# Moving seven small loads to other queues, adding three filler products, and a new hand-off order in an S5 scan and MLP kernel

## The chip, the cores and the metric

The kernel runs on one core of one Trainium2 chip. A core has four compute engines that run their own instruction streams: TensorE (PE, matrix products into PSUM), VectorE (DVE), ScalarE (ACT) and GpSimd (POOL). A fifth, SyncE (SP), only issues transfers and waits. Transfers between the device's memory and the on-chip buffer are issued from the stream of SP, ACT or POOL and carried by DMA engines. Engines meet at semaphores. The metric is the device time of one execution in microseconds; the median of several executions is compared.

## The reference, cut to what matters

```python
xn = layernorm(x)                                   # x: 1 x 2048 x 448, bfloat16
# A: a diagonal complex recurrence over the 2048 positions
Lam_bar = exp(exp(log_dt) * Lam);  B_bar = ((Lam_bar - 1) / Lam)[:, None] * Bmat
Bu = einsum("bld,pd->blp", xn, B_bar)
h[t] = Lam_bar * h[t-1] + Bu[t]
s = 2 * real(einsum("blp,dp->bld", h, Cmat)) + xn * Dskip
# B: an MLP over a second layernorm
g = silu(gelu(layernorm(xn) @ w1 + b1) @ w2 + b2)   # w1: 448 x 1792, w2: 1792 x 448
out = x + s * g
```

## The kernel before, in words

The 2048 positions are cut into four groups of 512 (g0 to g3), each of two blocks of 256. For each group the kernel makes the two normalised inputs (transposed by DMA into `xnT` for the scan and `xn2T` for the MLP), the first MLP product with w1 and its GELU (`mm1_phase`, lines 650 to 670, the GELU on ACT at line 668), the second with w2 and its SiLU (`mm2`, lines 778 to 790), the scan's input products (`bu_phase`, 679 to 722), the scan itself on DVE (`ssm`, 736 to 770), the scan's output products (`yt`, 794 to 829) and the sum with x (`out_dma`, `out_pe`). The contraction over 448 rows is done in 64-row halves that run side by side in the PE.

The first group is special. Its MLP products run for block 0 as soon as x's first rows have come (`first_stats`, `first_apply`), and for block 1 after that, in pieces of 256 columns; a pair of PSUM banks holds two of w1's column blocks, there are three such pairs, and ACT has to apply the GELU to a pair before the PE can fill it again. Ahead of the first products the PE runs filler products on constants (`dummies`, lines 376 to 378: `n` products of `cols` columns into a bank that nobody reads) and a few tiny products that turn rows of parameters into columns: `parameters` (475, 476), `b1_columns` (549, 550) and `skip_columns` (555, 556, which takes the rows of D and b2 that are loaded at line 355).

w1 is loaded in four column chunks (`ldw1`, 335 to 339): rows 0 to 383 of a chunk, then the remainder, rows 384 to 447, as a DMA of its own, and a copy `w1c` of a part of it to other partitions. All of them are issued by SP in the kernel before, and so are the rows of D and b2.

What runs where and when is written out. Every operation is a numbered task of a `Plan`, in the order in which the program adds it. `ORDER` (line 154) is a hand-off order of all task numbers; each engine's stream is that list with the other engines' tasks left out, and a task waits only for the tasks whose data it needs (`emit`, 99 to 146). So an engine that waits at the head of its stream holds everything behind it. Some tasks may run on either of two engines (`either`, 65 to 70: `small` is GpSimd or VectorE, `copy` is ScalarE or VectorE); those whose numbers stand in `SECOND` (line 174) take the second one.

Places that the prediction's steps use: `ln_scale` (416 to 434, the scale and offset of a group's layernorm: ten short chained operations on DVE, or five with a power on GpSimd), `ln_apply` (436 to 445, lines 443 on DVE and 444 on ACT), the sine of the parameters (`sine`, 492 to 498, ten short chained operations), `tables` (564 to 584: range reduction of the rotation table at 566 to 570, its absolute value at 572, five sines on ACT at 580, the decay table `dk` at 583), `lb` (609 to 616) and `bt` (618 to 622), which make and transpose the scan's input matrices `BT`, and `combine` (588 to 597).

Of the kernel before, what the change touches and what calls it, by code (L numbers as in the profile page):

```python
# [148 lines left out]
def dram_ap(t, offset, ap):  # L149
    return bass.AP(tensor=t.tensor, offset=offset, ap=ap)  # L150
# [1 line left out]


ORDER = [int(k) for k in """
# [18 lines left out]
""".split()]  # L173
SECOND = [int(k) for k in """
26 29 32 56 60 69 83 90 113 115 172 173 175 177 178 180 181 182 202 204 205 207 208 209 210 212 214 216 218 220 222 234 236 238 240 244 246 256 258
270 277 278 280 324 338 349 360 361 364 365 409 443 444 445 446 471 472 473 474 475 487 489 527 528 529 542 549 551 560 575
""".split()]


# [18 lines left out]
def bass_recurrent_scan__ssm_conv_s5__mixer_channel_mlp__prompt_kernel(  # L198
# [11 lines left out]
    L, D, F = 2048, 448, 1792  # L210
# [6 lines left out]
    with ExitStack() as es:  # L217
        def SB(name, shape, dtype=BF):
            return es.enter_context(nc.sbuf_tensor(name, shape, dtype))
# [12 lines left out]
        w1_sb = SB("w1_sb", [128, 4, F])  # L232
# [9 lines left out]
        drows = vrows[64:66, 64:512]  # L242
# [54 lines left out]
        def pe(fn, reads=(), writes=(), split=False):  # L297
            kb.add("pe", fn, reads, writes, split=split)

        def copy(pairs, rd, wr):  # L300
            kb.either(("act", [lambda e, o=o, i=i: e.activation(o, i, ACT.Copy) for o, i in pairs]),  # L301
                      ("dve", [lambda e, o=o, i=i: e.tensor_copy(o, i) for o, i in pairs]), rd, wr)

        with nc.Block():
# [17 lines left out]
            def ld(eng, o, i, writes, reads=()):  # L322
                kb.dma(eng, o, i, reads=reads, writes=writes)
# [4 lines left out]
            def ldx(b0, n, reads=()):  # L328
                ld("sp", x_all[:, b0:b0 + n, :, :], dram_ap(A_x, b0 * 256 * D, [[2 * D, 128], [256 * D, n], [D, 2], [1, D]]),
                   [f"x{b}" for b in range(b0, b0 + n)], reads)  # L330
# [4 lines left out]
            def ldw1(c):  # L335
                a, w = CH[c][0] * 128, CH[c][1] * 128
                ld("sp", w1_sb[:, 0:3, a:a + w], dram_ap(B_w1, a, [[F, 128], [128 * F, 3], [1, w]]), [f"w1_{c}"])
                ld("sp", w1_sb[64:128, 3, a:a + w], dram_ap(B_w1, 384 * F + a, [[F, 64], [1, w]]), [f"w1r_{c}"])
                copy([(w1_sb[0:64, 3, a:a + w], w1_sb[64:128, 2, a:a + w])], [f"w1_{c}"], [f"w1c_{c}"])

            for par in range(2):
                ld("sp", x_all[:, 0, par, :], dram_ap(A_x, par * D, [[2 * D, 128], [1, D]]), [f"x0p{par}"])
            ldx(1, 1)
            ldw1(0)
            ld("act", brows[0:3, :], dram_ap(B_b1, 256, [[512, 3], [1, 512]]), ["br0"], ["br"])
            ld("act", brows[3:4, 0:256], dram_ap(B_b1, 0, [[256, 1], [1, 256]]), ["br1"], ["br"])
            for c in range(1, 4):
                ldw1(c)
# [3 lines left out]
            for c, (a, n) in enumerate(CH):  # L352
                ld("sp", w2_sb[:, a:a + n, :], dram_ap(B_w2, a * 128 * D, [[n * D, 128], [D, n], [1, D]]), [f"w2_{c}"])
            for i, vec in enumerate((A_Dskip, B_b2)):
                ld("sp", drows[i:i + 1, :], dram_ap(vec, 0, [[D, 1], [1, D]]), [f"dbr{i}"])
            ldx(2, 2)
            def xk(b):
                return [f"x{b}"] if b else ["x0p0", "x0p1"]
# [17 lines left out]
            def dummies(n, rd=(), bank=3, cols=256):  # L376
                wide = nc.const_aps.tensor_like(1.0, xn_sb[:, 0, 0:cols])
                pe([lambda e: e.matmul(psum[:, bank, 0:cols], one, wide, start=True, stop=True) for _ in range(n)], list(rd), [f"ps{bank}"])
# [169 lines left out]
            def b1_columns():  # L548
                pe([lambda e, k=k: e.matmul(psum[:, 4, 2 + k:11 + k:4], brows[0:4, k:512:4], ident[32:36, 32:35], start=True, stop=True) for k in range(4)]
                   + [lambda e, k=k: e.matmul(psum[:, 4, k:k + 1], brows[0:4, k:256:2], ident[32:36, 35:36], start=True, stop=True) for k in range(2)],  # L550
                   ["br", "br0", "br1", "ident"], ["ps4"])
                copy([(b1f[:], psum[:, 4, 0:14])], ["ps4"], ["b1f"])
# [119 lines left out]
            def mm1_run(g, b, js, pairs):  # L672
                for j in js:
                    mm1_phase(g, b, j, pairs[j - js[0]], False)
                    if j > js[0]:
                        mm1_phase(g, b, j - 1, pairs[j - 1 - js[0]], True)
                mm1_phase(g, b, js[-1], pairs[js[-1] - js[0]], True)
# [205 lines left out]
            dummies(1, ["st0"])  # L883
            first_apply(0)
            b1_columns()
            mm1_run(0, 0, range(6), (0, 1, 2, 0, 1, 2))
            first_apply(1)
            mm1_run(0, None, range(6, 7), (0,))
# [83 lines left out]
```

## Time and profile before

| | us |
|---|---|
| median of three executions without a profile | 148.27 (147.64 to 148.87) |
| the profiled execution, its own time | 148.68 |
| its span, from the first instruction to the last | 146.9 |
| TensorE busy in the span | 140.0 (95%) |
| VectorE busy | 130.7 (89%) |
| ScalarE busy | 102.8 (70%) |
| GpSimd busy | 23.9 (16%) |

The time of an execution is the span and 1.8 us around it. Rows of the profile give a start and a duration in us, the engine (PEld is the PE's load of weights, SPq and ACTq are issues of transfers), the line of the kernel, the operation, the tiles as out<-in and a count; in brackets stands the idle time of the engine before it and what ended that. In a table of windows, each engine has its busy time and the number of its instructions, then come the PE's granted clock, the busy share of the DMA engines and the rate of transfers.

### The profile page before, as it was taken

What the parts mean: (1) busy time and instruction counts of PE and PEld (TensorE: products, weight loads), DVE (VectorE), ACT (ScalarE), POOL (GpSimd) and SP (SyncE); (2) the same over time, 40 slices, a digit from 0 to 9 for tenths busy, and PEclk for the clock granted to TensorE, in tenths of its full rate; (3) what the DMA queues carried; (4) which work ended last, traced back from release to release, by engine and by line L of the source; (5) the groups of instructions that cost most, each with busy time, mean ns of one, the idle gap of its engine ahead of it and who ended that gap; (6) DMA issues with size and microseconds to landing.
All of it is one profiled execution on the core that took longest, in us unless ns stands there. A gap on an engine that the chain in (4) does not pass through costs nothing.

```text
span 146.9 us, 3570 instructions
## 1 busy us (share of the span) xinstructions
PE 140.0 (95%) x1421; PEld 90.2 (61%) x1427; DVE 130.7 (89%) x284; ACT 102.8 (70%) x188; POOL 23.9 (16%) x83
## 2 busy tenths in 40 slices
PE   7789999999999999999999999999999999999990
PEld 2577774454455485466758555887775668564860
DVE  2989999999587999999999999496999999999891
ACT  3667999988799766999989773615768997064200
POOL 2630777710000000060500000000000600000000
PEclk9977999999999999999999999999999999999998
DMA  4799996999589791000000018917440010005404
GB/s 114 219 253 275 393 230 127 167 251 184 105 170 230 146 112 35 2 4 0 4 0 0 0 22 160 212 38 147 84 155 0 0 63 4 18 0 107 182 10 125
DMA packets 38850, 15.98 MB, mean 109 GB/s; under 512 B 33193, under 2 KB 38450, under 8 KB 38834
## 3 DMA queue, kind: packets, MB, share of 16 engines
q1 hardware_dynamic: 38276, 15.52, 47.6%
q10 hardware_dynamic: 558, 0.24, 0.6%
q8 instruction: 11, 0.18, 0.5%
q14 instruction: 5, 0.04, 0.1%
HBM read 5.86 MB, written 1.84 MB: 52 GB/s over the span
## 4 chain that ended last, share of the span: by engine, by line
PE 86%; ACT 4%; SPq 2%; DMA 2%; issue 1%; DVE 1%; DVEq 0%
PE psum L662 28%; PE psum L784 24%; PE psum L691 14%; PE psum L806 7%; PE psum L807 6%; PE psum L787 4%; ACT gT L668 3%; SPq L78 2%; DMA w_sb<-in_B_w_dram 2%; PE psum L814 2%; ACT xn_sb L444 1%; DVE Bn L862 1%; ACT tmp L595 0%; PE psum L815 0%; PE psum L856 0%
## 5 line engine op out<-in xcount | busy, mean ns | idle before, releaser
L662 PE MATMUL psum<-xn2T,w_sb 64*128 64x512 bf16 (+1 forms) x476 | 48.3, 349 | 0.7 <-DMA w_sb<-in_B_w_dram 0.4
L668 ACT ACTIVATE gT<-psum,b1f 128x512 bf16<-128x512 f32 (+1 forms) x68 | 37.3, 615 | 4.9 <-PE psum L662 3.9
L784 PE MATMUL psum<-gT,w_sb 128*128 128x512 bf16 x162 | 36.3, 379 | 0.6 <-issue 0.3
L662 PEld LDWEIGHTS psum<-xn2T,w_sb 64*128 64x128 bf16 x476 | 26.5, 111 | 16.6 <-PE psum L662 1.9
L784 PEld LDWEIGHTS psum<-gT,w_sb 128*128 128x128 bf16 x168 | 16.2, 98 | 18.9 <-issue 0.6
L691 PE MATMUL psum<-xnT,BT 64*128 64x256 bf16 x392 | 24.4, 269 | 0.0
L691 PEld LDWEIGHTS psum<-xnT,BT 64*128 64x128 bf16 x392 | 18.8, 94 | 6.2 <-issue 0.8
L790 ACT ACTIVATE g_sb<-psum,db 128x512 bf16<-128x512 f32 (+1 forms) x16 | 9.8, 627 | 10.2 <-PE psum L787 4.6
L750 DVE TENSOR_TENSOR_SCAN s_w<-vs,dk 128x1048 f32<-128x1048 bf16 (+1 forms) x8 | 16.4, 2061 | 0.2
L444 ACT ACTIVATE xn_sb<-x_all,lnw 128x448 bf16<-128x448 bf16 (+2 forms) x20 | 13.2, 696 | 0.1
L827 DVE SCALAR_TENSOR_TENSOR tmp<-xnT,db,psum 128x512 f32<-128x512 bf16 (+1 forms) x17 | 10.8, 650 | 2.5 <-PE psum L815 1.8
L301 ACT ACTIVATE vs<-s_w 64x258 bf16<-64x258 f32 (+2 forms) x11 | 6.5, 611 | 6.7 <-DVE s_w L750 6.6
L806 PE MATMUL psum<-hx,CZ 128*128 128x256 bf16 x84 | 10.9, 275 | 0.0
L807 PE MATMUL psum<-Bn,CQ 128*128 128x256 bf16 x84 | 10.8, 273 | 0.0
L466 ACT ACT_TABLE_LOAD x8 | 10.3, 1283 | 0.3
L301 ACT ACTIVATE ue<-psum 128x512 bf16<-128x512 f32 (+1 forms) x14 | 7.1, 548 | 4.5 <-PE psum L691 4.5
L806 PEld LDWEIGHTS psum<-hx,CZ 128*128 128x128 bf16 x84 | 8.0, 98 | 2.4 <-ACT u_sb L301 0.4
L807 PEld LDWEIGHTS psum<-Bn,CQ 128*128 128x128 bf16 x84 | 8.0, 98 | 1.6 <-issue 0.4
L829 DVE TENSOR_TENSOR t<-tmp,g_sb 128x512 bf16<-128x512 f32 (+1 forms) x14 | 8.4, 626 | 0.0
L301 ACT ACTIVATE u_sb<-psum 128x256 bf16<-128x256 f32 (+1 forms) x14 | 6.1, 508 | 2.8 <-PE psum L691 2.8
L443 DVE TENSOR_SCALAR xn_sb<-x_all,lnw 128x384 bf16<-128x384 bf16 (+2 forms) x20 | 6.1, 353 | 1.8 <-ACT xn_sb L444 1.7
L364 DVE BATCH_NORM_STATS2 lnst<-x_all 128x6 f32<-128x448 bf16 x12 | 7.0, 614 | 0.0
(158 smaller groups left out, 174.4 us busy)
## 6 DMA issues: line engine op xcount, KB each, us to landing
x_all<-in_A_x_dram SPq DMA_DIRECT2D x3, 448.0 KB, 4.7
w_sb<-in_B_w_dram SPq DMA_DIRECT2D x3, 448.0 KB, 7.1
out_dram<-Bn SPq DMA_DIRECT2D x6, 224.0 KB, 2.9
w_sb<-in_B_w_dram SPq DMA_DIRECT2D x3, 384.0 KB, 4.3
Bn<-in_A_B_im_dram SPq DMA_DIRECT2D x1, 336.0 KB, 7.6
Bn<-in_A_B_re_dram SPq DMA_DIRECT2D x1, 336.0 KB, 7.9
x_all<-in_A_x_dram SPq DMA_DIRECT2D x2, 112.0 KB, 2.1
x_all<-in_A_x_dram SPq DMA_DIRECT2D x1, 224.0 KB, 2.6
```

The source lines that it names most:

```text
L301: kb.either(("act", [lambda e, o=o, i=i: e.activation(o, i, ACT.Copy) for o, i in pairs]), ("dve", [lambda e, o=o, i=i: e.tensor_copy(o, i ...
L444: ("act", [lambda e, o=o, i=i: e.activation(o, i, ACT.Identity, bias=nb, scale=rs) for o, i in parts]),
L466: kb.add("act", lambda e: e.preload_act_table_set(what), reads, writes, sem=name)
L662: return lambda e: e.matmul(dst(bk[k]), w1_sb[rows, d, fcol(2 * j + k)], rhs[rows, d], start=not second and n == 0, stop=second and n == 3)
L668: act(lambda e, k=k, fi=fi: e.activation(gT[:, gb, fi, cols], psum[:, bk[k], cols], ACT.Gelu_apprx_tanh, bias=b1f[:, fi:fi + 1]), ["b1f", ...
L691: fns.append(lambda e, rows=rows, bank=bank, m=m, o=o, n=n: e.matmul(psum[:, bank, c * NK:(c + 1) * NK].rearrange("p (b c) -> p b c", b=2) ...
L750: dve(lambda e, so=so, vi=vi, di=di: e.tensor_tensor_scan(so, vi, di, 0.0, ALU.add, ALU.mult), ["v", "vl", "vz", "dk", "dk01"] + ["v3"] * ...
L784: pe([lambda e, fi=fi: e.matmul(psum[:, bk, :], w2_sb[:, fi, 128 * j:128 * j + 128], gT[:, gb, fi, :], start=fi == 0, stop=fi == NF - 1) f ...
L790: act(lambda e: e.activation(g_sb[:, gb, 512 * j:512 * j + n], psum[:, bk, 0:n], ACT.Silu, bias=b2c[:, j:j + 1]), [f"ps{bk}", "db", f"Ws{g ...
L806: pe([lambda e, k=k: e.matmul(par(psum[:, bk, :], 1), CZ[:, k, cols], halves(hx[:, hb, k, 1:NK + 1]), start=k == 0, stop=k == 6) for k in ...
L807: fns = [lambda e, k=k: e.matmul(par(psum[:, bk, :], 0), CQ[:, k, cols], halves(hz[:, hb, k, :]), start=not by_pe and k == 0, stop=not by_ ...
L827: dve([lambda e, o=o, p=p, x=x, d=d: e.scalar_tensor_tensor(out=v(o), in0=x, scalar=d, in1=v(p), op0=ALU.mult, op1=ALU.add) for o, p, x, d ...
```

## The change

Three edits are written in the code, and the two lists are new.

```diff
-                ld("sp", w1_sb[64:128, 3, a:a + w], dram_ap(B_w1, 384 * F + a, [[F, 64], [1, w]]), [f"w1r_{c}"])
+                ld("act", w1_sb[64:128, 3, a:a + w], dram_ap(B_w1, 384 * F + a, [[F, 64], [1, w]]), [f"w1r_{c}"])
...
-                ld("sp", drows[i:i + 1, :], dram_ap(vec, 0, [[D, 1], [1, D]]), [f"dbr{i}"])
+                ld("pool", drows[i:i + 1, :], dram_ap(vec, 0, [[D, 1], [1, D]]), [f"dbr{i}"])
...
             b1_columns()
+            dummies(3, cols=512)
             mm1_run(0, 0, range(6), (0, 1, 2, 0, 1, 2))
...
 ORDER = [int(k) for k in """
-9 11 16 17 18 44 14 15 13 42 24 10 22 12 4 23 360 2 93 94 95 96 97 106 0 101 1 45 92 105 107 46 47 98 111 49 41 99 102 25 50 19 20 100 66 27 34 110 3
...
+2 3 11 25 14 15 5 0 12 44 10 6 13 9 4 1 45 16 93 94 22 95 23 17 18 24 19 96 97 106 46 98 20 99 48 41 111 101 92 105 100 47 107 108 109 42 53 36 28 112
...
 SECOND = [int(k) for k in """
-26 29 32 56 60 69 83 90 113 115 172 173 175 177 178 180 181 182 202 204 205 207 208 209 210 212 214 216 218 220 222 234 236 238 240 244 246 256 258
...
+21 26 29 32 48 50 57 59 60 63 66 73 75 76 80 83 85 89 90 110 173 177 179 180 182 203 204 206 209 210 211 213 215 217 219 221 223 232 235 237 241 243
...
```

The added filler task has number 116, so a task that had a number from 116 on now has the next one. With that taken into account the lists differ as follows, as far as the prediction speaks of it.

- ScalarE's stream: the remainder of w1's chunk 1 is its first issue, ahead of the three rows of parameters; the remainder of chunk 0 comes behind the second pair of logarithm and exponential of `first_stats`, those of chunks 2 and 3 right after the exponential of log_dt. SP's stream keeps w1's upper rows, in the order chunk 1, 0, 2, 3.
- GpSimd's stream: the rows of D and b2 are issued behind its constants. It gets the `ln_scale` of group 0 (before on VectorE), further down that of group 2, and two more of the four products of the identity with D (line 562).
- From ScalarE to VectorE: the copies of w1's chunk 0 (`w1c_0`) and of the first transposed half block, two of the four `ln_apply` of group 0's scan input. From VectorE to ScalarE: the copy of the second transposed half block, the column b1, one `ln_apply` of group 1's MLP input.
- From GpSimd to VectorE: the sine of the parameters, the wrap before it (`wrap`, 489 to 491) and a dozen short operations on parameters; four such go the other way.
- ScalarE's absolute value (line 501) stands ahead of the first GELU instead of behind the eighth. Behind the last GELU of group 0 it has first one `ln_apply` of group 1 (line 444), then the SiLU table, then the absolute value of line 572.
- VectorE's stream: the copies of w1's chunks 1 and 2, `dk` and one of the four operations of line 570 come later; the third is behind the `ln_scale` of group 1.
- SP's stream: x's blocks 4 and 5 are issued behind the transposes of `xnT` for group 0 instead of ahead of them; the three transposes of `BT` come in the order 2-5-6, 0-3, 1-4 with a load of x in between.
- The PE's stream up to group 1's second product is the same but for the filler products; from there on neighbouring tasks change places in some thirty spots. In the last group the output's block 3 comes last instead of block 2.

More of the change, by code (lines that the diff above doesn't have):

```diff
@@ L154 @@
 ORDER = [int(k) for k in """
[18 rows of a table removed]
[18 rows of a table added]
 """.split()]
 SECOND = [int(k) for k in """
-26 29 32 56 60 69 83 90 113 115 172 173 175 177 178 180 181 182 202 204 205 207 208 209 210 212 214 216 218 220 222 234 236 238 240 244 246 256 258
-270 277 278 280 324 338 349 360 361 364 365 409 443 444 445 446 471 472 473 474 475 487 489 527 528 529 542 549 551 560 575
+21 26 29 32 48 50 57 59 60 63 66 73 75 76 80 83 85 89 90 110 173 177 179 180 182 203 204 206 209 210 211 213 215 217 219 221 223 232 235 237 241 243
+245 247 249 257 261 271 272 277 279 281 323 339 340 352 353 365 366 430 444 445 446 447 473 474 475 488 490 530 531 543 550 561 576
 """.split()]
```

34 rows, old and new, of the table ORDER are left out of this document.

## The prediction

> **What bounds the kernel now.** I began with the chain of waits, to see where the time lies before the PE is fed without a break; then the windows of half a microsecond over the start, then ScalarE's timeline. The chain in order of time, rows with start and length:
>
> ```profile
> 4.67 3.47 DMA w_sb<-in_B_w_dram
> ...
> 18.53 3.03 PE psum L662 x50
> 21.57 0.16 issue
> 21.73 9.01 PE psum L784 x41
> 30.74 1.65 PE psum L787 x28
> 32.39 6.22 PE psum L662 x55
> ```
>
> The first products of the MLP wait until 8.14 for the small remainder of w1's chunk 0, the ninth transfer that SP issues. The first GELU stage keeps the PE until 21.57; from 21.73 to 32.39 the second product of group 0 runs without a gap, and so on. Behind that hardly anything is free, and windows that I put over the rest show it:
>
> ```profile
> 32.30:57.20 24.90, 24.45 (x254) 13.90 (x255) 21.41 (x61) 20.01 (x34) 0.00 (x0) 1.00 0.84 153
> ...
> 45.30:142.40 97.10, 96.75 (x999) 63.92 (x1003) 90.66 (x150) 65.46 (x117) 7.33 (x14) 1.00 0.30 63
> ```
>
> From 45.3 to 142.4 the PE is busy for 96.75 of 97.10 us. A reordering there has 0.35 us to win. What can be won is in front of 45, and it stays won if nothing else is late. The start in windows (PE, PEld, DVE, ACT, POOL, granted clock, DMA share, GB/s):
>
> ```profile
> 6.50:7.00 0.50, 0.13 (x5) 0.04 (x2) 0.27 (x2) 0.46 (x2) 0.43 (x3) 1.00 0.71 149
> 7.00:7.50 0.50, 0.00 (x1) 0.03 (x2) 0.47 (x3) 0.13 (x1) 0.50 (x3) 1.00 0.62 162
> ...
> 8.50:9.00 0.50, 0.50 (x14) 0.50 (x10) 0.50 (x5) 0.50 (x1) 0.14 (x1) 1.00 0.86 221
> ...
> 9.50:10.00 0.50, 0.50 (x10) 0.42 (x7) 0.45 (x2) 0.14 (x1) 0.42 (x3) 0.50 0.98 266
> ...
> 12.50:13.00 0.50, 0.44 (x8) 0.20 (x6) 0.45 (x2) 0.50 (x2) 0.00 (x0) 0.91 1.08 262
> ```
>
> The PE is idle around 7 us, and soon after its products begin the granted clock is halved until about 12.5. Who pays for that is seen on ScalarE, which has to drain every pair of banks:
>
> ```profile
> 7.80 1.28 ACT L466 ACT_TABLE_LOAD   x1
> 9.86 0.84 ACT L668 ACTIVATE gT<-psum,b1f 128x256 bf16<-128x256 f32 x2 [0.78 <-DVE w_sb L302]
> 11.31 1.69 ACT L668 ACTIVATE gT<-psum,b1f 128x256 bf16<-128x256 f32 x4 [0.61 <-PE psum L662]
> 13.47 0.84 ACT L668 ACTIVATE gT<-psum,b1f 128x256 bf16<-128x256 f32 x2 [0.47 <-PE psum L662]
> ...
> 14.30 0.75 ACT L444 ACTIVATE xn_sb<-x_all,lnw 128x448 bf16<-128x448 bf16 x1
> 14.96 5.13 ACT L668 ACTIVATE gT<-psum,b1f 128x256 bf16<-128x256 f32 x12
> 20.41 1.97 ACT L668 ACTIVATE gT<-psum,b1f 128x256 bf16<-128x256 f32 x5 [0.33 <-PE psum L662]
> 22.26 0.77 ACT L444 ACTIVATE xn_sb<-x_all,lnw 128x448 bf16<-128x448 bf16 x1
> 22.91 0.48 ACT L668 ACTIVATE gT<-psum,b1f 128x256 bf16<-128x256 f32 x1
> ```
>
> The 26 GELUs run from 9.86 to 23.39, 13.53 us. Their own work is 0.84 + 1.69 + 0.84 + 5.13 + 1.97 + 0.48 = 10.95; the rest is waits for the PE (0.61 + 0.47 + 0.33 = 1.41) and two copies of 0.75 and 0.77. From 14.96 ScalarE sets the pace, not the PE.
>
> **The change part by part.** *Filler products.* Three of 512 columns stand behind b1's columns. At full clock 41 products of 512 took 9.01, 0.22 each: 0.66 us in a stretch where the PE sat idle. They cost nothing while the PE waits there anyway; with the cover gone, 0.66 (1.3 at the halved clock). If they hold the clock, the waits of 0.61 and 0.47 go: up to 1.08.
>
> The Trainium skill ("TensorE: Matmul & The Clock Gate", section "Why this matters for your kernels") says that only idle gaps of over about 3 us cool the PE. By that the filler would save nothing. This trace disagrees: the gap around 7 us was far shorter, and 0.50 followed.
>
> *ScalarE ahead of the table.* It gets four issues. Rows for them and for what follows:
>
> ```profile
> 3.41 2.40 SPq L78 DMA_DIRECT2D w_sb<-in_B_w_dram  x4
> ```
>
> ```profile
> 4.93 0.20 ACT L389 ACTIVATE lnw<-lnw 128x1 f32<-128x1 f32 x1
> 5.54 0.60 ACT L301 ACTIVATE xn2T<-psum 128x512 bf16<-128x512 bf16 x1 [0.41 <-PE psum L407]
> 6.06 0.21 ACT L485 ACTIVATE cw<-cw 128x8 f32<-128x8 f32 x1
> 6.46 0.30 ACT L392 ACTIVATE lnw<-lnmv,eps 128x2 f32<-128x2 f32 x1 [0.19 <-DVE lnmv L386]
> ```
>
> An issue is 2.40 / 4 = 0.60. The first one delays the rows of parameters, which the PE's early queue takes in order; I put that at nothing to 0.4, since fillers stand behind them. The other three begin at 5.13 and end, with one exponential of 0.20 between, at 7.1. Then logarithm and exponential (0.53), the copy of the second half block (0.60 instead of VectorE's 0.41), 0.21 and about 0.15, and the table from 8.6 to 9.9, absolute value to 10.1. The first GELU so stands at 10.05 against 9.86: the wait of 0.78 behind the table covers most of it. The PE can begin when that copy ends, 8.25, which is the old 8.27. The remainder itself is no longer ninth in one queue: issued at 5.2, with the old 3.47 as an upper bound it lands at 8.7, and with nothing ahead of it in ScalarE's queue well before; I take 8.2. D's rows on GpSimd replace two SP issues; its cost has no row, and GpSimd has nothing else between its constants and 4.8, so I take nothing.
>
> *The GELU run.* One copy instead of two lies in it: 10.05 + 10.95 + 0.75 = 21.75 if the PE keeps ahead, 1.64 before the old 23.39; with all waits for the PE back it is 23.2.
>
> *VectorE.* Its stretch from the second block's apply to the end of group 1's scale decides what ScalarE does next:
>
> ```profile
> 7.51 1.12 DVE L402 TENSOR_SCALAR xn_sb<-x_all,lnmv,lnw 128x384 bf16<-128x384 bf16 x4
> ...
> 11.98 0.16 DVE L508 TENSOR_SCALAR cw<-cw 128x4 f32<-128x4 f32 x1
> ...
> 17.94 0.66 DVE L302 COPY dk<-cw 128x1024 f32<-128x1024 f32 x1
> ...
> 18.79 0.17 DVE L423 TENSOR_SCALAR lnw<-lnmv 128x4 f32<-128x4 f32 x1
> ...
> 20.60 0.17 DVE L433 SCALAR_TENSOR_TENSOR lnw<-lnmv,lnw 128x8 f32<-128x8 f32 x1
> ```
>
> Ten chained short operations take 20.77 - 18.79 = 1.98, so 0.2 each. Added: wrap 0.6, sine 2.0, seven short ones at 0.16, three half-block applies at about 0.4, chunk 1's copy 0.3: 5.2. Removed or put behind: the scale of group 0 2.0, `dk` 0.66, three products with D 0.7, one of line 570 0.45, two or three short ones 0.4: 4.2. So 1.0 more than the old 13.26, from 7.7: the scale ends at 22.0, not 20.77. ScalarE's apply of group 1 waits for it behind the GELUs, 0.25 us.
>
> ```profile
> 25.00 1.28 ACT L466 ACT_TABLE_LOAD   x1
> ...
> 31.30 0.67 ACT L790 ACTIVATE g_sb<-psum,db 128x512 bf16<-128x512 f32 x1
> 32.43 0.47 ACT L790 ACTIVATE g_sb<-psum,db 128x256 bf16<-128x256 f32 x1 [0.47 <-PE psum L787]
> ```
>
> From the table at 25.00 to 31.97 ScalarE works 6.97; in the new order the table starts at 22.7 and line 572 (some 0.95) lies behind it: 30.6. The PE ends the first stage 1.07 before the last GELU, as before (23.39 - 21.57 - 0.75): 20.7, and with 0.16 and the 10.66 of the second product it ends at 31.5. So the PE is later than ScalarE, and the last SiLU ends at 32.0 instead of 32.90. That is 0.9 won.
>
> *Behind that.* VectorE makes the scan's matrices about 1.2 later; SP's transposes, how long those of `BT` take to land, and their first reader:
>
> ```profile
> 27.67 3.96 SPq L77 DMA_TRANSPOSE xnT<-xn_sb  x1
> 32.41 3.60 SPq L77 DMA_TRANSPOSE BT<-Bn  x1
> ```
>
> ```profile
> DMA to landing us min/median/max: 4.4/5.9/7.2
> ```
>
> ```profile
> 42.61 0.82 PE L691 MATMUL psum<-xnT,BT 64*128 64x256 bf16 x12
> ```
>
> The three transposes of `BT` take at most 7.2 from issue to landing, so 42.6 - 39.6 = 3.0 is left, of which 0.9 + 1.2 = 2.1 is used. x's blocks 4 and 5 now stand behind the 3.96 of `xnT`'s transposes, come 3 to 4 us later and may hold VectorE for 1 to 2; it was idle for 24.90 - 21.41 = 3.5 between 32.3 and 57.2. So nothing, with thin cover. The end: 0 to 0.3 for the smaller last block; I take 0.
>
> **Sum.** 148.68 - 0.9 = 147.8 for the profiled execution. It was 0.41 above the median of 148.27, so the median should come to 147.4. A difference of under 1% (1.5 us) can't be told from none here.
>
> **The rivals.**
> *A, more is won.* If VectorE isn't late (its operations overlap more than I count) and the table isn't either, the whole 13.53 - 11.70 = 1.83 arrives: 146.4. For it: ScalarE set the pace from 14.96. Against it: VectorE's added 1.0.
> *B, the clock is halved all the same*, since the filler covers only 0.66 of the gap. The 1.08 returns, the GELUs end at 22.8, the PE at 21.8, the second product at 32.6: 0.2 later than before, 148.5. The page named above would also have the filler do nothing.
> *C, slower: VectorE and GpSimd hand the parameters to and fro.* Half of that chain is now on each, and each hand-over blocks VectorE's queue ahead of group 1's scale:
>
> ```profile
> POOL cw L505 <- DVE cw L505: 1.6, 2, 1.2
> ```
>
> The longest was 1.2. With three such, 3.6 less the 1.0 that they may share with other waits, the scale ends 2.6 later, at 24.6; it decides from 22.9 on, where the 0.9 is eaten. 148.27 - 0.9 + 2.6 = 150.0.
> *D, slower: the row of D from GpSimd comes late.* The PE's queue has D's columns ahead of all MLP products; past 8.2 each microsecond is one of the run. 3 us late gives 150.4. The window before 4.8 speaks against it.
>
> **How the numbers follow.** My forecast 0.49, with 146.9 to 148.3 as its own range; A 0.28, B 0.08, C 0.10, D 0.05. Faster by over 1% (under 146.8) is A and 0.04 of the forecast: 0.32. Slower (over 149.75) is C and D: 0.15. The rest, 0.53, is within 1%. The range from 145.9 to 149.4 leaves out the tails of A and most of C and D.
>
> **What would show it.** The filler: clock 1.00 in all windows from 8 to 13, and no wait for the PE in the GELU run. The table: start near 8.6, first GELU near 10.0. VectorE: the end of group 1's scale near 22.0, with ScalarE's apply right behind. The last SiLU of group 0 near 32.0. The forecast is wrong if clock 0.50 stands behind 9 us, if the PE waits at the columns of D, if that scale ends after 23, or if the first product of the scan's input waits for a transpose.

## The result, and the profile after

The changed kernel takes 149.62 us (median of 12 executions, 148.40 to 152.04), the kernel before 147.95 beside it (12 executions, 147.17 to 148.87). The ratio is 1.0106, with a 95% interval from 1.0066 to 1.0145: slower by 1.0 to 2.1 us, where 147.4 was forecast, 0.9 less than before. Ratios, here and below, leave out disturbed executions, so that they can differ from the quotient of the medians beside them. The profiled execution took 149.44, with a span of 147.6, and is close to its median.

The timeline of the PE in the changed kernel (start, duration, operation, tiles, count, and in brackets the idle time ahead and what ended it):

```profile
5.28 0.21 PE L475 MATMUL psum<-ident,dk 3*128 3x3 bf16 x3 [1.73 <-DMA dk<-in_A_Lambda_re_dram]
...
6.39 0.63 PE L407 MATMUL psum<-ident,xn_sb 128*128 128x128 bf16 x4
6.81 1.06 PE L378 MATMUL psum<-const-bfloat16-1.0 128*128 128x256 bf16 x4
7.67 0.63 PE L407 MATMUL psum<-ident,xn_sb 128*128 128x128 bf16 x4
8.23 0.30 PE L549 MATMUL psum<-ident,dk 4*128 4x3 bf16 x4
...
8.52 0.82 PE L378 MATMUL psum<-const-bfloat16-1.0 128*128 128x512 bf16 x3
9.28 0.22 PE L555 MATMUL psum<-ident,dk 2*128 2x2 bf16 x3
9.43 0.19 PE L556 MATMUL psum<-ident,dk 2*64 2x2 bf16 x2
10.63 2.89 PE L662 MATMUL psum<-xn2T,w_sb 64*128 64x256 bf16 x48 [1.01 <-issue]
```

Two waits are new. The first columns of parameters stand 1.73 for the row of Lambda_re, and everything behind them on the PE is late; then the first MLP product (L662) comes at 10.63, not 8.27. Who is late is seen on ScalarE's timeline of the same kernel (ACTq are its issues of transfers), with SP's row of w1's chunks 2 and 3 at its end:

```profile
0.79 0.58 ACTq L78 DMA_DIRECT2D w_sb<-in_B_w_dram  x1
...
2.36 0.27 ACTq L78 DMA_DIRECT2D dk<-in_A_Lambda_re_dram  x1
...
4.44 0.25 ACTq L78 DMA_DIRECT2D dk<-in_B_b_dram  x1
5.67 0.18 ACT L478 ACTIVATE cw<-psum 128x12 f32<-128x12 f32 x1 [1.03 <-PE psum L476]
...
6.07 0.52 ACTq L78 DMA_DIRECT2D w_sb<-in_B_w_dram  x1
...
9.14 1.28 ACT L466 ACT_TABLE_LOAD   x1
```

```profile
3.82 1.11 SPq L78 DMA_DIRECT2D w_sb<-in_B_w_dram  x2
```

And the page's list of transfers, from which the flight of the remainder of chunk 0 is read (the only one of 32 KB; the last column is the time from issue to landing):

```profile
w_sb<-in_B_w_dram ACTq DMA_DIRECT2D x1, 32.0 KB, 4.5
```

The row of Lambda_re is issued at 2.36 instead of 1.61, behind the remainder of chunk 1. ScalarE's queue has its first operation on parameters (L478) behind it, and so the second logarithm and, behind that, the issue of chunk 0's remainder: 6.07. With 4.5 of flight it lands at 10.6, and the PE starts at 10.63. (That row of the PE says `issue`, so the profile itself names nothing that it waited for; the landing is worked out from the issue and the flight.)

What the rest makes of it, in the GELU run and the chain of waits:

```profile
12.02 3.16 ACT L668 ACTIVATE gT<-psum,b1f 128x256 bf16<-128x256 f32 x8 [1.36 <-PE psum L662]
...
21.45 2.52 ACT L668 ACTIVATE gT<-psum,b1f 128x256 bf16<-128x256 f32 x6
23.84 1.11 ACT L444 ACTIVATE xn_sb<-x_all,lnw 128x384 bf16<-128x384 bf16 x2
24.96 1.28 ACT L466 ACT_TABLE_LOAD   x1
...
33.30 0.47 ACT L790 ACTIVATE g_sb<-psum,db 128x256 bf16<-128x256 f32 x1
```

```profile
22.59 9.01 PE psum L784 x41
31.61 1.65 PE psum L787 x28
```

```profile
45.30:142.40 97.10, 96.67 (x1005) 64.29 (x1005) 90.18 (x151) 65.95 (x119) 11.08 (x17) 1.00 0.32 63
```

The GELU run is shorter, 23.97 - 12.02 = 11.95 instead of 13.53, but begins 2.16 later. (The page's chain leads to the PE's next products, at 13.67, through VectorE's sine, which the change has moved there. No product needs the sine. What these products need is the second pair of banks, and the fourth GELU, from 12.02 on at 3.16 / 8 = 0.40 each, ends at 13.6.) The second product of group 0 starts at 22.59 instead of 21.73, 0.86 late, and hardly anything is added behind it: from 45.3 to 142.4 the PE is as full as before (96.67 and 96.75), and the two profiled executions differ by 149.44 - 148.68 = 0.76.

Between the medians it is 1.67, and that needs a sentence on the kernel before: of 29 of its executions beside the second set of experiments, 16 had a mean granted clock of 0.996 or more and took 147.04 to 147.80, ten had 0.98 to 0.99 and took 148.00 to 148.92. The one that was profiled (0.984, 148.68) is of the second kind. The mean clock doesn't sort all executions, though: beside all the experiments together, 89 executions, the 32 with 0.98 to 0.99 all took 148.00 or more, but of the 46 with 0.996 or more nine did so too. Against one of the first kind the changed kernel would have the whole late start to show, 10.63 - 8.27 = 2.36; that is an estimate, since none of these was profiled.

### The profile page after: what moved, and what is told of

Read it like the earlier page. It is cut to its first block, busy times and chain, and to the rows that moved or that the text cites. A ratio compares the mean times of both kernels' runs of the same rounds, so it can differ in the third digit from the quotient of the medians.

```text
span 147.6 us, 3573 instructions
## 1 busy us (share of the span) xinstructions
PE 139.4 (94%) x1425; PEld 90.0 (61%) x1430; DVE 131.6 (89%) x283; ACT 102.1 (69%) x189; POOL 26.4 (18%) x75
## 4 chain that ended last, share of the span: by engine, by line
PE 87%; DVE 5%; DMA 2%; issue 1%; ACTq 1%; ACT 1%; DVEq 0%
PE psum L662 28%; PE psum L784 24%; PE psum L691 15%; PE psum L806 7%; PE psum L807 6%; PE psum L787 4%; PE psum L814 2%; DMA dk<-in_A_Lambda_re_dram 2%; DVE xn_sb L402 1%; ACTq L78 1%; DVE Bn L862 0%; DVE s_w L566 0%; DVE ang L497 0%; DVE w_sb L302 0%; DVE ang L496 0%
## 5 line engine op out<-in xcount | busy, mean ns | idle before, releaser
L662 PE MATMUL psum<-xn2T,w_sb 64*128 64x512 bf16 (+1 forms) x476 | 46.3, 339 | 1.3 <-issue 1.0
L662 PEld LDWEIGHTS psum<-xn2T,w_sb 64*128 64x128 bf16 x476 | 25.5, 108 | 16.6 <-PE psum L662 1.4
L750 DVE TENSOR_TENSOR_SCAN s_w<-vs,dk 128x786 f32<-128x786 bf16 (+1 forms) x8 | 16.4, 2060 | 0.1
L759 POOL TENSOR_TENSOR ang<-s_w,ang 128x16 f32<-128x16 f32 x2 | 1.1, 562 | 41.6 <-ACT s_w L757 41.6
L423 POOL TENSOR_SCALAR lnw<-lnmv 128x4 f32<-128x4 f32 x3 | 1.3, 437 | 34.4 <-DVE lnmv L368 33.4
```

What stands on the lines that cost most here:

```text
L662: return lambda e: e.matmul(dst(bk[k]), w1_sb[rows, d, fcol(2 * j + k)], rhs[rows, d], start=not second and n == 0, stop=second and n == 3)
L750: dve(lambda e, so=so, vi=vi, di=di: e.tensor_tensor_scan(so, vi, di, 0.0, ALU.add, ALU.mult), ["v", "vl", "vz", "dk", "dk01"] + ["v3"] * ...
```

## The experiments

Numbers in the list `ORDER`: 14, 15 and 13 are the rows of parameters, 4 is ScalarE's first operation with its table load, 22 and 23 the rows of b1 (chunks of four and of two column blocks are kept apart; 23 is the short second one), 25 and 20 the remainders of w1's chunks 1 and 0, 95 the first logarithm. In the kernel before, 23 stood ahead of 95; in the changed one it stands behind it.

| kernel | median (executions) | before beside it | ratio, 95% interval |
|---|---|---|---|
| rows_first | 150.70 (12) | 148.38 | 1.0096, 1.0047 to 1.0145 |
| rem0_early | 151.34 (6) | 148.38 | 1.0194, 1.0136 to 1.0253 |
| both_early | 150.84 (6) | 148.38 | 1.0158, 1.0105 to 1.0211 |
| rem_on_sp | 147.43 (12) | 148.38 | 0.9961, 0.9924 to 0.9999 |
| b1_rows_first | 147.21 (12) | 147.75 | 0.9968, 0.9935 to 1.0002 |
| after_nofill | 151.05 (6) | 147.75 | 1.0239, 1.0187 to 1.0291 |
| rem_on_sp_nofill | 148.22 (12) | 147.75 | 1.0005, 0.9973 to 1.0038 |
| before_filler | 147.46 (12) | 147.75 | 0.9981, 0.9950 to 1.0013 |
| b1_early_rem_late | 150.59 (6) | 148.21 | 1.0129, 1.0085 to 1.0173 |
| before_rem_act | 151.96 (6) | 148.21 | 1.0240, 1.0207 to 1.0274 |
| before_dpool | 149.30 (12) | 148.21 | 1.0050, 1.0013 to 1.0088 |
| rem_sp_b1_early | 147.17 (6) | 148.21 | 0.9921, 0.9895 to 0.9948 |
| chunks_behind | 149.37 (10) | 147.73 | 1.0078, 1.0039 to 1.0117 |
| chunks_behind_b | 152.64 (4) | 148.36 | 1.0297, 1.0228 to 1.0367 |

**First set: is it ScalarE's issues?** Three kernels move one or two issues within ScalarE's stream, the fourth gives the remainders back to SP. The texts below number the theories: 1, ScalarE's issues make the loss, the late rows of parameters included; 2, only the flight of chunk 0's remainder does; 3, the new order or another part of the change does.

rows_first:

```diff
-2 3 11 25 14 15 5 0 12 44 10 6 13 9
+2 3 11 14 15 5 0 12 44 10 6 13 25 9
```

> The changed kernel with one number moved: ScalarE issues the remainder of chunk 1 behind the three rows of parameters instead of ahead of them. Theory 1 (the loss is made by ScalarE's issues: the row of Lambda_re lands at 5.14 instead of 3.31, what ScalarE does behind it is late, the remainder of chunk 0 is issued at 6.07 and lands at 10.54): the PE's first transposes of parameters move from 5.28 to about 3.6, the issue of chunk 0's remainder from 6.07 to about 4.9, and if its flight keeps its 4.5 it lands near 9.4; the first MLP product at 9.4 instead of 10.63, the median near 148.5. Theory 2 (only the flight of the remainder in a loaded queue counts, the rows of parameters are covered by fillers): landing past 10 all the same, 149.3 or more. Theory 3 (the new order behind 23 us costs the time): 149.6, whatever the start does.

rem0_early:

```diff
-10 6 13 9 4 1 45 16
+10 6 13 20 9 4 1 45 16
...
-46 98 20 99
+46 98 99
```

> The changed kernel with one other number moved: ScalarE issues the remainder of chunk 0 right behind the rows of parameters, at about 2.7 instead of 6.07; the rows stay as late as they were. Theory 1 and theory 2: it lands by 8, and the first MLP product waits for the copy of the second half block that ends at 8.96, so it comes at 9.0 instead of 10.63, the table at 9.1 and the first GELU near 10.5 instead of 12.02; the PE keeps 1.0 to 1.6 of that, median 148.0 to 148.6. Theory 3 (new order behind 23): 149.6.

both_early:

```diff
-2 3 11 25 14 15 5 0 12 44 10 6 13 9
+2 3 11 14 15 5 0 12 44 10 6 13 20 25 9
...
-46 98 20 99
+46 98 99
```

> The changed kernel with both moves: ScalarE issues the three rows of parameters, then the remainder of chunk 0, then that of chunk 1. Theory 1: the PE's transposes of parameters near 3.6, first MLP product near 8.3, table near 8.2, first GELU near 10.0, the GELU run 11.9 as in the changed kernel, so the second product of group 0 starts near 20.7 instead of 22.59; median 147.0 to 147.7, below the kernel before or level with it. Theory 2 (rows are covered): the same as with the remainder of chunk 0 alone, 148.0 to 148.6. Theory 3 (new order behind 23): 149.0 or more.

rem_on_sp:

```diff
-                ld("act", w1_sb[64:128, 3, a:a + w], dram_ap(B_w1, 384 * F + a, [[F, 64], [1, w]]), [f"w1r_{c}"])
+                ld("sp", w1_sb[64:128, 3, a:a + w], dram_ap(B_w1, 384 * F + a, [[F, 64], [1, w]]), [f"w1r_{c}"])
```

with 25 behind 24, 20 behind 19, 28 behind 27 and 31 behind 30 in `ORDER`.

> The changed kernel with w1's four remainders issued by SP again, in the order of the kernel before; filler products, rows of D on GpSimd and the new order stay. Theory 1 and 2: rows of parameters at 3.3, the remainder of chunk 0 lands near 8, first MLP product near 8.3, median 147.0 to 147.7. Theory 3 (new order, filler or GpSimd's rows cost the time): 149 or more.

With the remainders on SP the loss is gone (0.9961), with the new order, the fillers and GpSimd's rows of D in place. So theory 3 falls. But theory 1 falls too in the form in which it stood: with the rows of parameters and both remainders early the kernel is no better than with them late. The PE of both_early shows why (its timeline, then its windows, with the granted clock third from the end):

```profile
5.58 0.40 PE L407 MATMUL psum<-ident,xn_sb 128*128 128x128 bf16 x4 [1.07 <-DVE xn_sb L402]
...
6.48 0.40 PE L407 MATMUL psum<-ident,xn_sb 128*128 128x128 bf16 x4
8.42 0.28 PE L549 MATMUL psum<-ident,dk 4*128 4x3 bf16 x4 [1.54 <-DMA dk<-in_B_b_dram]
...
8.68 1.46 PE L378 MATMUL psum<-const-bfloat16-1.0 128*128 128x512 bf16 x3
...
10.38 4.67 PE L662 MATMUL psum<-xn2T,w_sb 64*128 64x256 bf16 x48
```

```profile
7.00:7.50 0.50, 0.00 (x0) 0.00 (x0) 0.50 (x4) 0.29 (x1) 0.17 (x1) 0.94 0.94 291
7.50:8.00 0.50, 0.00 (x0) 0.00 (x0) 0.44 (x4) 0.47 (x3) 0.50 (x4) 0.50 1.09 366
...
13.50:14.00 0.50, 0.50 (x10) 0.33 (x6) 0.47 (x2) 0.15 (x1) 0.50 (x1) 0.50 1.06 398
...
14.50:15.00 0.50, 0.50 (x12) 0.28 (x6) 0.50 (x3) 0.50 (x3) 0.50 (x3) 1.00 1.10 287
```

Nothing waits for the remainder any more. The PE now waits for the second row of b1, which ScalarE issues behind its first logarithm. In those 1.54 the clock falls to a half, the fillers take 1.46 instead of 0.82, and the half clock lasts until past 14. By the 0.94 of its window it fell at about 7.44 (an estimate), when the wait was only 0.56 old; the PE had been idle for 1.07 ahead of 5.58 too, so the 1.54 alone need not be the cause. In rem0_early the same wait is 2.30. In rows_first it is 1.14, a wait for the remainder follows, and the first 48 products take 5.07:

```profile
7.46 0.27 PE L549 MATMUL psum<-ident,dk 4*128 4x3 bf16 x4 [1.14 <-DMA dk<-in_B_b_dram]
...
10.00 5.07 PE L662 MATMUL psum<-xn2T,w_sb 64*128 64x256 bf16 x48 [0.67 <-issue]
```

The changed kernel has that late row too; it lay hidden, since its PE was later still. This is theory 4.

**Second set: both late rows repaired, and the fillers taken apart.** b1_rows_first leaves all four remainders on ScalarE. As in both_early, the rows of parameters come first (9 is VectorE's clearing of the place where b1's rows land):

```diff
-2 3 11 25 14 15 5 0 12 44 10 6 13 9 4 1 45 16 93 94 22 95 23 17
+2 3 11 9 14 15 5 0 12 44 10 6 13 4 22 23 20 25 1 45 16 93 94 95 17
...
-46 98 20 99
+46 98 99
```

> The changed kernel with ScalarE's first issues in another order and nothing else: three rows of parameters, then the first table load, and in its shade both rows of b1, the remainder of chunk 0 and that of chunk 1; only then the first logarithm. The four remainders stay on ScalarE. Theory 4 (the loss is what stands behind other work of ScalarE's stream: first the remainder of chunk 0, and once that is early, b1's second row behind the first logarithm, whose columns the PE has ahead of the fillers and of the MLP products): b1's second row lands by 6 instead of 8.28 with both remainders early, the PE goes from the second half block's transposes to b1's columns without a gap, clock 1.00 in all windows from 7, first MLP product near 9.0, median 147.0 to 147.8. Rival (64 rows issued by ScalarE cost the time by themselves, or ScalarE's own work is later by the four issues): the first logarithm a microsecond later than 3.88, first MLP product after 10, 149 or more.

Its PE and its first GELUs:

```profile
6.31 0.30 PE L549 MATMUL psum<-ident,dk 4*128 4x3 bf16 x4
...
6.59 0.82 PE L378 MATMUL psum<-const-bfloat16-1.0 128*128 128x512 bf16 x3
7.82 0.21 PE L555 MATMUL psum<-ident,dk 2*128 2x2 bf16 x3 [0.41 <-ACT cw L485]
...
8.08 2.94 PE L662 MATMUL psum<-xn2T,w_sb 64*128 64x256 bf16 x48
```

```profile
9.47 3.21 ACT L668 ACTIVATE gT<-psum,b1f 128x256 bf16<-128x256 f32 x8
```

The first product comes at 8.08, earlier than the 9.0 expected, at the full rate; the median is in the range given. The engine that issues is not the cost: the place in its stream is.

after_nofill and rem_on_sp_nofill take the fillers out, before_filler puts them into the kernel before; the list is renumbered and nothing else moved.

```diff
             b1_columns()
-            dummies(3, cols=512)
             mm1_run(0, 0, range(6), (0, 1, 2, 0, 1, 2))
```

> The changed kernel without its three filler products; all else stays. If the fillers hold the clock and stand in idle time: the first MLP product stays at 10.6, where the remainder of chunk 0 lands; the PE is idle from 8.6 or so to 10.6, the granted clock is 0.50 for one or two windows of 3.4 us behind that, and the GELU run of 11.95 gets back 1 to 1.6: median 150.6 to 151.2. If a gap of 2 us doesn't cool the PE: 149.6, as with them.

> The changed kernel with the remainders on SP again, and without the three filler products, which there ran at half rate from 7.33 to 8.79 with nothing else to wait for but the first MLP product behind them. If the fillers only take time: first MLP product near 7.6 instead of 9.03, median 146.0 to 146.6. If the fillers hold the clock: products begin earlier but at half rate for some microseconds, the granted clock is 0.50 in one window of 3.4 us, and 1.2 to 1.7 are lost again: median 147.4 to 148.4, level with the kernel before.

> The kernel before with the three filler products of 512 columns behind b1's columns and nothing else. They start at 6.63, in the wait for D's row (7.50) and for chunk 0's remainder (8.14). If they hold the clock: no 0.50 from 9.17 to 12.58, the first GELU a little later (9.9 to 10.2), the waits of 0.61 and 0.47 gone; median 147.0 to 147.6, 0.4 to 1.0 below the kernel before. If they run at half rate, 1.4, they end at 8.1 and delay nothing either. If the clock falls all the same: level with the kernel before, within 0.3.

In the changed kernel the fillers are worth 1.4 between the medians (151.05 against 149.62), and some 2.0 by the two ratios: without them 48 products take 4.41 where they took 2.89.

```profile
10.28 4.41 PE L662 MATMUL psum<-xn2T,w_sb 64*128 64x256 bf16 x48 [1.42 <-issue]
```

The window of 0.50 that was expected isn't recorded there; the half rate is read from the durations alone. With the remainders on SP the fillers stand on the path and, in the profiled execution, run at half rate. They lose nothing all the same: 0.9961 with them, 1.0005 without, and as the intervals overlap, a gain isn't shown either. Without them the products begin at 7.92, but the clock is 0.50 from 8.5 to 11.5. The timeline of rem_on_sp:

```profile
7.33 1.46 PE L378 MATMUL psum<-const-bfloat16-1.0 128*128 128x512 bf16 x3
...
9.03 3.21 PE L662 MATMUL psum<-xn2T,w_sb 64*128 64x256 bf16 x48
```

In the kernel before the fillers change the median by less than can be told (0.9950 to 1.0013); the profile of before_filler has no 0.50 in the first 25 us. rem_on_sp_nofill, at 1.0005, is also the measurement of the new order and GpSimd's rows together: nothing beyond 0.4% either way.

**Third set: the table of two by two, and single parts.** b1_early_rem_late is b1_rows_first with 20 behind 98 again.

```diff
-13 4 22 23 20 25 1 45
+13 4 22 23 25 1 45
...
-46 98 99
+46 98 20 99
```

> The kernel with b1's rows in the shade of the first table load, which gave 147.21, with one number moved: the remainder of chunk 0 is issued behind the second logarithm and exponential again, as in the changed kernel. With the two runs that had the remainder early and b1's second row late (151.34, 150.84) and the changed kernel (both late, 149.62) it completes a table of two by two. Theory 4 (two waits in a row on the PE's stream; taking one away only shows the other): the remainder is issued at 5.0 to 5.5 and lands at 9.3 to 10, the PE waits for it with its fillers done, first MLP product 9.5 to 10.1, median 148.6 to 150.2. Rival (only b1's second row counts): level with 147.2.

```profile
7.88 0.19 PE L556 MATMUL psum<-ident,dk 2*64 2x2 bf16 x2
10.08 2.89 PE L662 MATMUL psum<-xn2T,w_sb 64*128 64x256 bf16 x48 [2.00 <-issue]
```

The rival falls. Four kernels issue the rows of parameters first; their ratios to the kernel before are: remainder and b1's row both late 1.0096 (rows_first), remainder early alone 1.0158 (both_early), b1's row early alone 1.0129, both early 0.9968. (With the rows of parameters late, it is 1.0106 for the changed kernel and 1.0194 for rem0_early.) Either repair alone wins nothing, since it leaves the other wait, and that wait is longer than in rows_first: 1.54 against 1.14 in both_early, where ScalarE issues the row of b1 at 4.89 instead of 4.25, and 2.00 against 0.67 here, where the PE is ready sooner.

The execution shown is the fastest of its six (149.08). It idled for 2.00 and went on at the full rate, 2.89 for 48 products, while the other five, at 150.46 to 151.72, have a mean granted clock of 0.982 to 0.989. So the length of a gap alone doesn't settle the clock.

before_rem_act changes the engine of line 338 in the kernel before, with 25 ahead of 14, 28 and 31 behind 47 and 20 behind 98. before_dpool changes the engine of line 355 alone, and the rows keep their numbers' places.

```diff
-                ld("sp", drows[i:i + 1, :], dram_ap(vec, 0, [[D, 1], [1, D]]), [f"dbr{i}"])
+                ld("pool", drows[i:i + 1, :], dram_ap(vec, 0, [[D, 1], [1, D]]), [f"dbr{i}"])
```

> The kernel before with one part of the change alone: the four remainders issued by ScalarE at the places that they have in the changed kernel (chunk 1 ahead of the rows of parameters, chunk 0 behind the second logarithm and exponential). Its own order, D's rows on SP, no filler. Theory 4: rows of parameters near 4.7 to 5.1 instead of 3.31, the remainder of chunk 0 issued after 5.5 and landed near 10, first MLP product after 10 and at half rate, as in the changed kernel without filler: median 150.0 to 151.5. If the new order is what costs: within 0.5 of the kernel before.

> The kernel before with the rows of D and b2 issued by GpSimd and nothing else. They land at 6 to 8 instead of 4.54 and 5.81; SP's chunks of w1 come 0.7 earlier. If D's row is on the path: PE's columns of D wait past 7.8, median up to 0.5 above the kernel before. If nothing waits for it: level, or 0.2 below since chunk 0's remainder lands earlier.

The remainders alone, at those places, make the kernel before slower by 2.4%: here the second logarithm is later still, the remainder of chunk 0 is issued only at 7.21, and the PE starts at 11.25, at half clock. The 151.96 is above the range given. In before_dpool the row of D stands in the middle of GpSimd's stream, is issued at 4.97 and holds the PE:

```profile
8.82 0.21 PE L555 MATMUL psum<-ident,dk 2*128 2x2 bf16 x3 [1.77 <-DMA dk<-in_A_Dskip_dram]
```

That costs 0.5% (0.1 to 0.9%). In the changed kernel it stands right behind the constants and is issued at 2.53, and nothing waits for it.

rem_sp_b1_early joins rem_on_sp with an early second row of b1:

```diff
-2 3 11 14 15 5 0 12 44 10 6 13 9 4 1 45 16 93 94 22 95 23 17
+2 3 11 9 14 15 5 0 12 44 10 6 13 4 22 23 1 45 16 93 94 95 17
```

> The changed kernel with both repairs in one: w1's remainders on SP, and b1's two rows behind the first table load's start, ahead of the first logarithm. Candidate for the best version. Against the remainders on SP alone (147.43): b1's second row lands near 4.7 instead of 6.78, but the columns stood right behind the second transposes there already, so at most 0.3 is won: 147.0 to 147.4. If b1's row made the fillers run cold there: the fillers take 0.83 instead of 1.46 and 0.6 is won in the executions in which they did.

It is the best of all and beats both kernels: 0.9921 of the kernel before, all six executions between 147.08 and 147.45, where the kernel before goes up to 149 and more. First product 7.87, fillers 0.82 instead of 1.46.

**Fourth set: why a flight of 4.5?**

```diff
-110 55 27 67 54 103 21 113 66 30 52
+110 55 67 54 103 21 113 66 52
...
-56 115 143 57
+56 115 143 27 30 57
```

> The changed kernel with SP's upper rows of chunks 2 and 3 issued behind the first transposes of xn2T instead of at 3.84 and 4.47; ScalarE's stream is untouched, so the remainder of chunk 0 is still issued near 6.07. If transfers of all queues share one road and land in about the order of their issues: with the two large chunks gone from in front of it, the remainder lands at 8.0 to 8.6 instead of 10.54, the PE no longer waits for it, and the first MLP product follows D's columns at 9.4 to 9.7. If the flight of 4.5 belongs to ScalarE's queue or to 64 rows of a remainder: it lands past 10 as before. The time has no sharp forecast, since chunk 2 then lands near 13 and may hold VectorE's copy of it: 148.5 to 151.

> The changed kernel with SP's upper rows of chunks 2 and 3 issued behind the first transposes of xn2T (near 10.5) instead of at 3.84 and 4.47; ScalarE's stream is untouched, so the remainder of chunk 0 is still issued near 6. If transfers of all queues share one road and land in about the order of their issues: with the two large chunks gone from in front of it, the remainder lands at 8.0 to 8.6 instead of 10.54, the PE no longer waits for it, and the first MLP product follows D's columns at 9.4 to 10.0. If the flight of 4.5 belongs to ScalarE's queue or to 64 rows of a remainder: it lands past 10 as before. The time has no sharp forecast, since chunk 2 then lands near 13 and may hold VectorE's copy of it: 148.5 to 151.

In chunks_behind the two numbers were put behind 142, a task of VectorE, and not behind 143, the transposes; no engine's stream changed by that. It is a second measurement of the changed kernel (1.0078, with a flight of 4.9) and says nothing on the question. chunks_behind_b has the diff above. Its list of transfers and its PE:

```profile
w_sb<-in_B_w_dram ACTq DMA_DIRECT2D x1, 32.0 KB, 2.0
```

```profile
9.40 0.19 PE L556 MATMUL psum<-ident,dk 2*64 2x2 bf16 x2
9.53 2.47 PE L662 MATMUL psum<-xn2T,w_sb 64*128 64x256 bf16 x42
14.70 0.52 PE L662 MATMUL psum<-xn2T,w_sb 64*128 64x256 bf16 x6 [2.71 <-DMA w_sb<-in_B_w_dram]
```

The same 32 KB from the same queue, issued at 5.92, take 2.0 instead of 4.5 once chunks 2 and 3 are not in front, and the first product follows D's columns without a wait. The mean busy share of the DMA engines between 6.0 and 8.5 is 1.03 to 1.12 in the changed kernel and at most 0.34 in chunks_behind_b. The transfers in front so explain most of the flight, but not its end: from 9.5 to 10.5, just before the landing, the share in the changed kernel is 0.13 and 0.03, and which engine was still at work is open. (The two chunks are then missing later: 2.71 of waiting, 152.64 in all, above the range given.)

## Why the prediction was wrong

**ScalarE ahead of the table: the step that failed.** Three of its terms.
- "Nothing to 0.4" for the rows of parameters. The PE's first transposes moved from 3.48 to 5.28, 1.8. Only 0.75 of it is the later issue; the rest is a longer flight, 2.78 in the changed kernel. That the transfers started by then made it longer is likely, but no run tests it for this row. The fillers behind them hid nothing, because they stand behind them in the same queue.
- The remainder "issued at 5.2", landing at 8.2 with 8.7 as a bound. It was issued at 6.07, since the logarithm ahead of it waited for those same rows, and flew 4.5, outside the bound. Giving it a queue with nothing ahead was taken for a short way. In the kernel before, SP issued it ahead of chunk 2; without remainders in its stream SP issues chunks 2 and 3 at 3.82 to 4.93, ahead of the remainder. The forecast counted what left SP's queue and not what moved up in it.
- A row was left out of the list of changes and of the sum: the second row of b1, moved by the new order behind the first logarithm (issue at 4.44 instead of 2.24). It cost nothing in the changed kernel only because the remainder was later, and 1.1 to 2.3 of the PE's time in the three kernels of the first set that left it there.

The first product so came at 10.63, not 8.25; the table at 9.14, not 8.6; the first GELU at 12.02, not 10.05.

The Trainium skill ("DMA: Bandwidth & Descriptors", section "Rules for kernel authors") says that spreading transfers over SP, ACT and GpSimd brings no bandwidth, because all run on the same 16 DMA engines, and only saves time of issue; in "Queues, rings and completion order", that the increment that reports a transfer lands only behind every earlier write of its DMA engine, across queues. The trace agrees: 4.5 with two large chunks of the other queue in front, 2.0 without.

**Filler products: right.** They cost nothing where they stood, held the clock, and the two waits of 0.61 and 0.47 in the GELU run shrank to 0.28 and 0.34. after_nofill puts 1.4 or more on them. What the forecast didn't see is that the kernel before pays for the clock only in some of its executions (ten of the 29 above, by their mean clock): the profiled one did, and its 13.53 were taken as the rule. So the gain that the sum began with was smaller for the median than for the profile, and the correction of 0.41 at the end of the sum stood for it only in part.

**The GELU run: right in length.** 11.70 was expected from first to last, 11.95 measured, with 0.28 + 0.34 of waits for the PE that the 11.70 had put at nothing. It only began 1.97 later than expected.

**D's rows on GpSimd: right** for their place in the changed kernel. Rival D, which had this row late, is a real mechanism, as before_dpool shows, but not what happened.

**VectorE: late by about as much as its start.** Group 1's scale ended at 22.94 instead of 22.0. Its row:

```profile
22.77 0.17 DVE L433 SCALAR_TENSOR_TENSOR lnw<-lnmv,lnw 128x8 f32<-128x8 f32 x1
```

VectorE's stretch began 1.0 late (8.50 against 7.51), behind the second half block. So rival C is out; the scale was ready for ScalarE's apply at 23.84 anyway.

**The last SiLU and what is behind it.** 33.77 instead of 32.0; 32.90 before, so 0.87 lost where 0.9 was to be won. The "nothing" put behind it was right: those 0.87 are about the difference of the profiled executions, 0.76, and neither x's blocks 4 and 5 nor the transposes of `BT` show as a wait of the PE.

**The rivals.** None had this mechanism. C and D made the kernel slower by other ways, and 0.15 for slower was too little; the slope of "past 8.2 each microsecond is one of the run" was priced for D's row and belonged to every small transfer ahead of the first product. The rule of the Trainium skill ("TensorE: Matmul & The Clock Gate", section "Why this matters for your kernels") that only gaps of over about 3 us cool the PE stays at odds with some runs: in both_early 1.54 of idle time was followed by 0.50. The 2.00 in the profiled execution of b1_early_rem_late, followed by the full rate, do fit it. What else decides, these runs don't show.

## What to carry to other kernels

When transfers leave a queue, list what moves up in that queue as well as what waits in the new one, and price a small transfer by the bytes that all queues issued ahead of it. Ahead of the first large product write down each small row that the PE's queue needs, with its landing: repairing one of two waits in a row can look like no gain or a loss, as in rem0_early, both_early and b1_early_rem_late. On an engine that computes too, issues belong in the shade of something long that waits for nothing, here the first table load.

## What the hardware showed that was not expected

The granted clock of the rows can say 1.00 while the PE runs at half rate. In rem_on_sp three products of 512 columns take 1.46 with 1.00 recorded throughout; in b1_rows_first the same three take 0.82. Likewise after_nofill. In all these cases no 0.50 had been recorded before, so the rate early in a run has to be read from durations.

The half clock comes and goes between executions of the same kernel, and fillers in the right place keep it away. Of the 29 executions of the kernel before named above, ten had a mean granted clock of 0.98 to 0.99; of the twelve of before_filler, the same kernel with three fillers, none had less than 0.993. Ten of these twelve took 147.02 to 147.73, the other two 148.11 and 148.78, so the spread is smaller and not gone, and that the median falls by it isn't shown.
